# Key-value sums with one column of ones for three heads, and warm-up products that read a preset constant

## The chip, the cores and the metric

The kernel runs on one core of one Trainium2 chip. The metric is the device time of one execution in microseconds (us). It computes, for 2048 tokens of width 640, a layer norm and then the sum of the input, a linear-attention block and a gated feed-forward block. All runs told of here are of the fast state, with a granted clock of 1.000 as recorded.

## The reference, cut to what matters

```python
xn  = layernorm(x)                                   # x: 1 x 2048 x 640, bf16
q, k, v = split(xn @ wqkv)                           # 32 heads of 20
phi_q = concat(softmax(q @ w_phi), softmax(-q @ w_phi))   # 40 features a head
phi_k = concat(softmax(k @ w_phi), softmax(-k @ w_phi))
kv = einsum("bhsf,bhsd->bhfd", phi_k, v)             # the key-value sums
z  = einsum("bhsf->bhf", phi_k)                      # their denominators
o  = (phi_q . kv) / (phi_q . z + 1e-6)
return x + o @ wo + (silu(xn @ w1) * (xn @ w3)) @ w2
```

## The kernel before

The program lists its instructions as streams (norms, projections, gated layer, outputs and so on). A list scheduler inside the program places them with estimated costs. What counts here are the key-value sums and the opening, which is about the first 7 us. An evacuation is the copy of a product's result out of the accumulators by ScalarE or VectorE. An idle product is one whose result nobody reads; it only keeps TensorE active.

A chunk of the sums is 120 feature rows, three heads of 40, and a product gives it the values of its three heads. To get `z` by the same product, each head's 20 values have a column of ones as their 21st. A chunk is therefore 63 columns wide, and there are 11 chunks by 16 row tiles = 176 products. The mask `FM` then keeps, for each row, only the block of its own head.

```python
v2 = new("v2", [128, T, H * 21], bf, RV)
...
memset("POOL", v2[:].rearrange("p t (h c) -> p t h c", c=21)[:, :, :, DH], 1.0)   # the ones
...
def keep_warm(n, rep, rate=2400):          # products that nobody reads
    for _ in range(rep):
        mm(bank(7, 128 * n), zero[:], zero[:].unsqueeze(1).to_broadcast([128, n, 128]), True, True,
           cost=128 * n / rate)

def warm_up():
    keep_warm(4, 8, 1200)
    keep_warm(1, 9, 1200)
...
def v_half(t, q, lo, hi):                  # values of one of the first four row tiles, half q
    ...
        mm(bank(k, 320), xnT[:, i, t * 128:(t + 1) * 128], WVK[:, i, 320 * q:320 * q + 320],
           i == 0, i == DC - 1)
...
def kv_sum(half, k):
    c0, c1 = ((0, 6), (6, QC))[half]
    for c in range(c0, c1):
        n = min(63, H * 21 - 63 * c)
        for t in range(T):
            m = min(128, (T - t) * 1280 - 120 * c)
            f = ekt[:].rearrange("p t f -> p (t f)")[:, 1280 * t + 120 * c:1280 * t + 120 * c + m]
            mm(bank(k, n, 63 * (c - c0))[0:m, :], f, v2[:, t, 63 * c:63 * c + n],
               t == 0, t == T - 1, True, 0.03)
    ...                                    # multiply by FM into KVc, add the epsilon
```

`zero` is a tile that VectorE clears as its first instruction, so the first idle product waits for VectorE.

The softmax here doesn't subtract the row's maximum and nothing guards it: scores larger than these inputs give would overflow.

## Time and profile before

| | before |
|---|---|
| time, median of 3 runs (range) | 266.49 us (266.28 to 266.64) |
| span in the profile | 265.3 us |
| TensorE busy | 259.9 us, 98% |
| VectorE, ScalarE, GpSimd busy | 69%, 40%, 36% |
| first idle product, first transpose | 1.05, 5.68 us |
| key-value products, first to the next other product | 81.37 to 86.48 us |

In a timeline each line has the start in us, the duration, the engine, the operation with what it writes and reads, the count, and in brackets the idle time before it and what ended that. PE is TensorE, and PEld its weight loads. The prediction below shows the lines of this kernel.

### The profile page before, as it was taken

The numbers are of one execution on the slowest core, as the hardware profiler recorded it, in microseconds if no ns is written. First come the engines' busy times: TensorE is split into PE (matmuls) and PEld (weight loads), VectorE is DVE, ScalarE is ACT, GpSimd is POOL, SyncE is SP. The second block draws the span as 40 slices with busy tenths as digits, with TensorE's granted clock in tenths as the row PEclk, the third lists the DMA queues.
The fourth block names the chain that finished last, engine by engine and source line by source line (L and its number), as shares of the span: only waits on it lengthen the run. The fifth ranks groups of instructions, "written<-read, shape, count | busy, mean of one in ns | idle before, by whom it ended". The sixth has DMA issues, their size and how long they took to land.

```text
span 265.3 us, 4446 instructions
## 1 busy us (share of the span) xinstructions
PE 259.9 (98%) x1764; PEld 145.5 (55%) x1792; DVE 183.9 (69%) x316; ACT 106.2 (40%) x226; POOL 95.9 (36%) x107
## 2 busy tenths in 40 slices
PE   7999999999999999999999999999999999999997
PEld 3555545565558556466565745555554544444773
DVE  4668999999796679696675858897979664221112
ACT  5646988799870442251405224434540410000000
POOL 4311587989997035207030430442333020000000
DMA  6996068822300990921515078445751540463431
GB/s 220 284 315 176 4 160 237 174 52 52 121 2 16 260 214 20 158 52 53 107 25 104 2 133 150 57 79 102 123 94 25 101 79 0 93 127 125 104 126 49
DMA packets 72069, 29.03 MB, mean 109 GB/s; under 512 B 60272, under 2 KB 72048, under 8 KB 72048
## 3 DMA queue, kind: packets, MB, share of 16 engines
q1 hardware_dynamic: 71904, 28.58, 47.8%
q8 instruction: 14, 0.23, 0.4%
q10 hardware_dynamic: 144, 0.16, 0.2%
q14 instruction: 7, 0.06, 0.1%
HBM read 11.49 MB, written 2.62 MB: 53 GB/s over the span
## 4 chain that ended last, share of the span: by engine, by line
PE 96%; DVE 1%; DMA 1%; issue 1%; POOL 0%
PE PS L104 96%; DMA x_tok<-in_A_x_dram 1%; DVE bst L104 1%; DVE x_tok L104 0%; POOL rstd L104 0%; DVE mv L104 0%; DVE xres L104 0%; DVE xnT L104 0%
## 5 line engine op out<-in xcount | busy, mean ns | idle before, releaser
L104 PE MATMUL PS<-xnT,w_s 128*128 128x512 bf16 x463 | 105.6, 379 | 1.0 <-issue 0.2
L104 PEld LDWEIGHTS PS<-xnT,w_s 128*128 128x128 bf16 x480 | 46.2, 98 | 50.9 <-DVE xnT L104 0.3
L104 POOL TENSOR_TENSOR eqt<-eqt,rS 128x600 bf16<-128x600 bf16 (+1 forms) x32 | 41.1, 1306 | 91.1 <-DVE rS L104 91.1
L104 ACT ACTIVATE th<-PS 128x512 f32<-128x512 f32 x48 | 28.6, 595 | 68.0 <-PE PS L104 67.9
L104 DVE SCALAR_TENSOR_TENSOR t<-th,PS 128x512 bf16<-128x512 f32 x48 | 32.2, 672 | 25.3 <-ACT th L104 25.3
L104 PE MATMUL PS<-WVK,xnT 128*128 128x512 bf16 (+3 forms) x255 | 45.1, 329 | 0.3
L104 POOL TENSOR_TENSOR ekt<-ekt,rS 128x640 bf16<-128x640 bf16 x32 | 39.8, 1276 | 4.9 <-DVE rS L104 4.9
L104 ACT ACTIVATE eqt<-PS 128x240 bf16<-128x240 f32 (+1 forms) x96 | 27.2, 348 | 25.9 <-PE PS L104 24.1
L104 PEld LDWEIGHTS PS<-WVK,xnT 128*128 128x128 bf16 x260 | 24.1, 98 | 19.4 <-ACT WVK L104 0.4
L104 DVE SCALAR_TENSOR_TENSOR hT<-t,PS 128x512 bf16<-128x512 bf16 x48 | 33.0, 687 | 1.7
L104 PE MATMUL PS<-w_s,hT 128*128 128x320 bf16 (+2 forms) x192 | 27.5, 299 | 0.0
L104 PE MATMUL PS<-hT,w_s 128*128 128x512 bf16 x115 | 27.3, 379 | 0.3
L104 DVE TENSOR_REDUCE S<-ekt 128x64 f32<-128x1280 bf16 x16 | 23.3, 1455 | 2.2 <-ACT ekt L104 2.2
L104 DVE TENSOR_REDUCE S<-eqt 128x66 f32<-128x1320 bf16 x16 | 24.2, 1515 | 0.4 <-ACT eqt L104 0.4
L104 PE MATMUL PS<-Wqp,xnT 128*128 128x360 bf16 (+1 forms) x160 | 24.3, 299 | 0.0
L104 ACT ACTIVATE ekt<-PS 128x640 bf16<-128x640 f32 x32 | 22.3, 702 | 1.3 <-PE PS L104 0.8
L104 PEld LDWEIGHTS PS<-w_s,hT 128*128 128x128 bf16 x192 | 18.3, 98 | 7.8
L104 DVE TENSOR_TENSOR xT<-PS,xT 128x512 bf16<-128x512 f32 x10 | 6.9, 689 | 22.0 <-PE PS L104 22.0
L104 PEld LDWEIGHTS PS<-hT,w_s 128*128 128x128 bf16 x120 | 11.7, 98 | 14.2
L104 PEld LDWEIGHTS PS<-Wqp,xnT 128*128 128x128 bf16 x160 | 15.2, 98 | 7.6
L104 DVE RECIPROCAL rS<-S 128x64 f32<-128x64 f32 (+1 forms) x32 | 17.9, 560 | 1.1
L104 DVE TENSOR_TENSOR xres<-PS,xres 128x640 bf16<-128x640 f32 (+2 forms) x9 | 6.7, 744 | 17.1 <-PE PS L104 17.1
(55 smaller groups left out, 176.9 us busy)
## 6 DMA issues: line engine op xcount, KB each, us to landing
w_s<-in_B_w_dram SPq DMA_DIRECT2D x6, 640.0 KB, 6.4
x_tok<-in_A_x_dram SPq DMA_DIRECT2D x3, 640.0 KB, 5.2
w_s<-in_B_w_dram SPq DMA_DIRECT2D x1, 1920.0 KB, 8.9
out_dram<-ot SPq DMA_DIRECT2D x2, 640.0 KB, 4.7
out_dram<-xres SPq DMA_DIRECT2D x7, 160.0 KB, 1.9
wo_s<-in_A_wo_dram SPq DMA_DIRECT2D x1, 800.0 KB, 5.0
WVK<-in_A_wqkv_dram SPq DMA_DIRECT2D x2, 320.0 KB, 4.0
xres<-in_A_x_dram SPq DMA_DIRECT2D x4, 160.0 KB, 5.8
```

The costliest lines, as they stand in the source:

```text
L104: o = _Op(eng, lambda: m(*args, **kw), r, w, cost)
```

## The change

The intent is to save two columns in each key-value product and to start TensorE without waiting for VectorE. A chunk gets one column of ones in front and then 3 x 20 values, so 61 columns. The mask copies the one denominator to its three heads' places. As a chunk must not straddle two evacuations, the halves of the value projection become 300 + 340 columns, and chunk 10 gets an evacuation of its own. The idle products read a constant that the preamble sets; there are three more of them. The scheduler gets conditions that keep an output behind the load that it adds to.

```diff
-    v2 = new("v2", [128, T, H * 21], bf, RV)
+    v2 = new("v2", [128, T, QC * 61], bf, RV)
+    v2c = v2[:].rearrange("p t (c n) -> p t c n", n=61)
...
-        memset("POOL", v2[:].rearrange("p t (h c) -> p t h c", c=21)[:, :, :, DH], 1.0)
+        memset("POOL", v2c[:, :, :, 0], 1.0)
...
+    one = nc.const_aps.tensor(1.0, [128, 512], bf)
...
-            mm(bank(7, 128 * n), zero[:], zero[:].unsqueeze(1).to_broadcast([128, n, 128]), True, True,
-               cost=128 * n / rate)
+            mm(bank(7, 128 * n), one[:, 0:128], one[:, 0:128 * n], True, True, cost=128 * n / rate)
...
-        keep_warm(1, 9, 1200)
+        keep_warm(1, 12, 1200)
...
+    VH = (0, 300, D)
...
+        if q:
+            evac(v2c[:, t, 10, 1:41], bank(k, 40, 300))
...
-            n = min(63, H * 21 - 63 * c)
+            n = 61 if c < QC - 1 else 41
...
-                mm(bank(k, n, 63 * (c - c0))[0:m, :], f, v2[:, t, 63 * c:63 * c + n],
-                   t == 0, t == T - 1, True, 0.03)
+                mm(bank(k, n, 61 * (c - c0))[0:m, :], f, v2[:, t, 61 * c:61 * c + n],
+                   t == 0, t == T - 1, True, 0.029)
...
-            stt(o[:, :, :, DH], i[:, :, :, DH], DEN_EPS / 2, m, ALU.add, ALU.mult)
+            stt(o[:, :, :, DH], i[:, :, 0].unsqueeze(2).to_broadcast([128, b - a, g]), DEN_EPS / 2, m,
+                ALU.add, ALU.mult)
...
-                    while done["o"] < t + 4 or done["h"] <= b:
+                    while done["o"] < t + 4 or done["h"] <= b or not done["x", b]:
```

More of the change, by code (lines that the diff above doesn't have):

```diff
@@ L546, in fold_mm @@
         evac(dst.rearrange("p (b c) -> p b c", c=320), bank2(k, 320))
+    VH = (0, 300, D)
     def v_out(t, q, k):
-        o = v2[:, t, 336 * q:336 * q + 336].rearrange("p (h c) -> p h c", c=21)[:, :, 0:DH]
-        i = bank(k, 320).rearrange("p (h c) -> p h c", c=DH)
+        o, i = v2c[:, t, 5 * q:5 * q + 5, 1:61], bank(k, 300).rearrange("p (c n) -> p c n", n=60)
         if t < 2 or t == 2 and q == 0:
@@ L561, in v_half @@
         for i in range(lo, hi):
-            mm(bank(k, 320), xnT[:, i, t * 128:(t + 1) * 128], WVK[:, i, 320 * q:320 * q + 320],
+            mm(bank(k, VH[q + 1] - VH[q]), xnT[:, i, t * 128:(t + 1) * 128], WVK[:, i, VH[q]:VH[q + 1]],
                i == 0, i == DC - 1)
@@ L572, in v_first @@
             for q in range(2):
-                mm(bank(2 + q, 320), xnT[:, i, 0:128], WVK[:, i, 320 * q:320 * q + 320], i == 0, i == DC - 1)
+                mm(bank(2 + q, VH[q + 1] - VH[q]), xnT[:, i, 0:128], WVK[:, i, VH[q]:VH[q + 1]],
+                   i == 0, i == DC - 1)
         if hi == DC:
@@ L594, in vk_features @@
                 mm(bank(k + q, hi - lo), xnT[:, i, t * 128:(t + 1) * 128], WVK[:, i, lo:hi], i == 0, i == DC - 1)
-        act(v2[:, t, :].rearrange("p (h c) -> p h c", c=21)[:, :, 0:DH],
-            PS[:, 512 * k:512 * k + D].rearrange("p (h c) -> p h c", c=DH), ACT.Copy)
+        act(v2c[:, t, :, 1:61], PS[:, 512 * k:512 * k + 660].rearrange("p (c n) -> p c n", n=60), ACT.Copy)
         k_exps(t, 512 * k + D)
@@ L650, in kv_sum @@
             o = KVc[:, c0 + a:c0 + b, 0:21 * g].rearrange("p c (g d) -> p c g d", d=21)
-            i = bank(k, 21 * g * (b - a), 63 * a).rearrange("p (c g d) -> p c g d", g=g, d=21)
+            i = bank(k, 61 * (b - a - 1) + 1 + DH * g, 61 * a)
             m = FM[:, a:b, 0:g]
-            tt("DVE", o[:, :, :, 0:DH], i[:, :, :, 0:DH], m.unsqueeze(3).to_broadcast([128, b - a, g, DH]), ALU.mult)
-            stt(o[:, :, :, DH], i[:, :, :, DH], DEN_EPS / 2, m, ALU.add, ALU.mult)
+            if b - a > 1:
+                i = i.rearrange("p (c n) -> p c n", n=61)
+            else:
+                i = i.unsqueeze(1)
+            tt("DVE", o[:, :, :, 0:DH], i[:, :, 1:1 + DH * g].rearrange("p c (g d) -> p c g d", d=DH),
+               m.unsqueeze(3).to_broadcast([128, b - a, g, DH]), ALU.mult)
+            stt(o[:, :, :, DH], i[:, :, 0].unsqueeze(2).to_broadcast([128, b - a, g]), DEN_EPS / 2, m,
+                ALU.add, ALU.mult)
     def q_tok(t, k):
@@ L738, in bass_parallel_sum__linear_kernel_hedgehog__glu_gated_swiglu__prompt_kernel @@
     done = dict.fromkeys(("w", "ln", "t", "f", "k", "v", "n", "kv", "p", "pn", "pt", "q", "o", "h", "m", "first", "t0"), 0)
-    done.update({("u", b): 0 for b in range(NB)})
+    done.update({(k, b): 0 for k in "ux" for b in range(NB)})
+    done["x", 0] = 1
     landed, pace, force = {}, [0], [False]
@@ L929, in outs @@
                 continue
-            while done["o"] <= t or done["h"] <= b:
+            while done["o"] <= t or done["h"] <= b or not done["x", b]:
                 yield None
@@ L938, in turns @@
         yield lambda: load_xT(1)
+        done["x", 1] = 1
         for b in xT:
@@ L945, in turns @@
                 yield lambda: P.dma("SP", xres[:], x_t[:, T - 4:T, :])
+                done["x", 3] = 1
             yield lambda b=b: store(b)
@@ L951, in late_loads @@
         yield lambda: load_xT(2)
+        done["x", 2] = 1
     def set_held(d):
```

## The prediction

> **What bounds the kernel now.** I read the page first: busy shares, then the chain that ended last.
>
> ```profile
> PE 259.9 (98%) x1764; PEld 145.5 (55%) x1792; DVE 183.9 (69%) x316; ACT 106.2 (40%) x226; POOL 95.9 (36%) x107
> ...
> PE 96%; DVE 1%; DMA 1%; issue 1%; POOL 0%
> ```
>
> TensorE is busy 98% of the span of 265.3 us, and the chain is TensorE for 96% of it. VectorE at 69% comes next, so only TensorE time, or time before TensorE's work can start, shortens the run. Busy time is no proof of full speed, however, because a matmul's record includes its pipeline latency. So I next read the chain in order of time, at its start and its end.
>
> ```profile
> 0.80 2.48 DMA x_tok<-in_A_x_dram
> ...
> 4.36 0.23 DVE mv L104
> ...
> 4.67 0.57 POOL rstd L104
> ...
> 6.69 0.36 DVE x_tok L104
> ...
> 7.09 4.56 PE PS L104 x41
> ...
> 258.86 4.58 PE PS L104 x33
> ...
> 263.46 0.29 DVE xres L104
> ```
>
> Up to 7.09 us the chain is the load of the first rows of x and their layer norm (DMA, VectorE, GpSimd, VectorE). From 7.09 to 263.44 it is TensorE without a break that matters: 256.35 us. Then come one addition and the last store.
>
> How close is that stretch to what TensorE can do? I take N/2.4 GHz + 2.5 ns from start to start (source below) and count the program's products: 480 of the gated layer by 215.8 ns = 103.6; values and keys 4.9 + 5.4 + 32.5 (4.9 being the 36 products of 320 columns left after 7.09, by 135.8); queries 80 x 271.7 ns = 21.7; outputs 36.7 + 32.3 + 4.6; weight folding 3.2; transposes 0.8; and about 5.0 each for the key-value sums and their readout. The sum is 255.7 us, plus some 0.17 us of latency of the last one. Against 256.35 us that leaves about 0.5 us of stalls in the whole stretch. No reordering can gain more than that 0.5 us.
>
> **The stages of the change**, in the timeline and in the views of the tiles:
>
> ```profile
> 0.37 0.10 POOL L1032 MEMSET const-bfloat16-1.0<- 128x1 bf16 x1
> ...
> 0.88 0.11 DVE L104 MEMSET zero<- 128x64 uint32 x1 [0.88 <-PEq L1032]
> ...
> 1.05 3.97 PE L104 MATMUL PS<-zero 128*128 128x512 bf16 x17 [1.05 <-DVE warm L104]
> ...
> 5.68 0.28 PE L104 MATMUL PS<-ident,x_tok 128*128 128x128 bf16 x2 [0.66 <-DVE x_tok L104]
> ...
> 81.37 5.27 PE L104 MATMUL PS<-v,ekt 128*128 128x63 bf16 x176
> ...
> 86.45 1.25 PEld L104 LDWEIGHTS PS<-Wqp,xnT 128*128 128x128 bf16 x10
> 86.48 1.52 PE L104 MATMUL PS<-Wqp,xnT 128*128 128x360 bf16 x10
> ```
>
> The idle products start at 1.05 us, when VectorE has written their zeros, and end at 5.02; the first useful one (a transpose) starts at 5.68, on VectorE's layer norm. The 176 key-value products fill 81.37 to 86.48 us: 5.11 us, with no gap at either edge.
>
> **What the Trainium skill says.** (1) "TensorE: Matmul & The Clock Gate", section "Wait — 56ns, not 53.3ns?": start to start N/1.2 GHz cold, N/2.4 GHz + about 2.5 ns warm, and never below about 25 ns. The trace agrees: the cold idle products of 512 columns start at 1.45, 1.88, 2.31 and 2.73 us, 0.43 apart. Of the key-value products, the 42-column ones (the last chunk) start some 25 ns apart (instants 86.09 and 86.29 read 8 products apart by that step), and the other 160 take (5.11 - 16 x 0.0253) / 160 = 29.4 ns against 63/2.4 + 2.5 = 28.8. So at 63 columns the width still counts, barely; at 42 the floor rules. (2) Same page, "What's actually happening": the clock opens after about 3.4 us of activity, in a window that runs freely. Here the 8th wide product, from 4.01 us, is already shortened: the gate opened around 4.3, 3.3 us after the first product. (3) "ScalarE: Activation LUTs", "What ACT_TABLE_LOAD costs": an ACTIVATE takes 186 ns + 0.833 N. The trace: 205 ns at 40 columns (page: 219), 438 at 320, 706 at 640.
>
> **The change part by part.**
> - Key-value products. 160 of 63 columns become 61, 16 of 42 become 41. The first saves 160 x 2 / 2.4 GHz = 0.133 us. The second saves nothing, being at the floor. TensorE is on the path here, so the 0.13 us is real, though only 0.05% of the run.
> - Masking. The two large multiplications (533 and 407 ns), the small one and the three sums of the denominators keep their element counts; only the strides and a repeated operand change. Nothing waits for them at once: the first reader of the result starts at 89.8 us, 2.2 us after the last. 0.
> - Value projection. For four row tiles the halves become 300 + 340 columns: 640 either way, so TensorE 0. Each second half needs one more evacuation of 40 columns, about 0.2 us on ScalarE or VectorE, four in all; the main one shrinks by 20 elements (17 ns). The other twelve copies take 660 columns instead of 640: 12 x 17 ns = 0.2 us on ScalarE, which is at 40%.
> - Ones. GpSimd's write of 512 strided elements takes 2.37 us; 176 elements cost about 0.8 by proportion. GpSimd is not waited for here. 0.
> - Idle products. They read a constant of the preamble, written by 0.47 us, so TensorE need not wait for VectorE: a start at about 0.8 to 0.85. Eight cold wide ones then end near 4.2, and twelve narrow ones (three more) by about 5.0 if warm, 5.5 if still cold. That is before 5.68, so they delay nothing. They gain nothing directly either: 5.68 is set by x and the layer norm, and the clock is full by then in this trace.
> - Order. The program places instructions by a simulated schedule with its own cost estimates. Those of the key-value products fall by 176 x 1 ns, the idle products end 0.04 us earlier in it by my count, and new evacuations appear, so the order may change after the opening. The new conditions before the outputs only keep an output from being placed ahead of the load it adds to.
>
> Sum: -0.13 us for the sums, about +0.1 for evacuations in the opening, -0.1 as the share of executions where an earlier, longer warm-up helps, and order between -0.3 and +0.4: about -0.2, so 266.3 us.
>
> **Rivals.**
> - The four small evacuations collide with the opening. There ScalarE and VectorE are close to the path: between 7.09 and 11.83 us TensorE has about 0.4 us of small stalls (0.15 on x_tok, 0.18 on xnT, about 0.3 before 11.83, part of it hidden). Each extra 0.2 us ahead of a copy of xnT can reach TensorE. For: ScalarE's value copies run without a break from 8.26 to 9.52, and a copy of xnT follows at once. Against: two of the four fall behind other work. Worst case +0.4: 266.7.
> - The clock. If the window opens one step earlier because the products start 0.25 us sooner, executions that open late gain up to about 1 us. For: three runs from 266.28 to 266.64. Against: the clock is already full at 5.68 here, and a start 0.25 us earlier matters in about 0.25/3.4 = 7% of phases. It would make 266.0 at most.
> - The order comes out worse, with TensorE waiting for a release of a bank or a late load. Against: VectorE and ScalarE have slack after the opening. It would make 267 to 268.
> - The products are bound by the weight load and not by their columns. Against: 42-column products with the same 128-column weights are 4 ns quicker. Then the gain is 0: 266.4.
>
> **Range and chances.** The certain part is -0.13, the limit for reordering gains is 0.5 us, runs of one kernel spread by 0.36 us, and the opening can lose 0.4. That gives 265.8 to 266.9. A change of 2% is 5.3 us; nothing here reaches it short of a broken schedule. Faster 0.005, within 2% 0.985, slower 0.01.
>
> **What would show it.** The key-value products should take about 4.97 us from the first to the product after them. The first idle product should start near 0.8, with the first transpose still at 5.7 and the chain entering TensorE near 7.1. TensorE's stretch from there should be about 256.2 us. I am wrong if that stretch moves by over 0.6 us, if the transposes move from 5.7, or if the sums stay at 5.1.

## The result, and the profile after

| | before | after |
|---|---|---|
| time, median of 6 runs (range) | 266.47 us (266.28 to 266.99) | 266.32 us (266.17 to 266.65) |
| span in the profile | 265.3 us | 265.1 us |

The ratio is 0.9994, with a 95% interval from 0.9981 to 1.0006. Ratios are the mean time of one kernel's fast runs over that of the other's of the same rounds, so not quite the ratio of the medians quoted. The interval allows anything from 0.5 us faster to 0.2 us slower. The traces, however, can be compared much more finely than the times.

First the busy line and the chain's shares on the page of the changed kernel:

```profile
PE 260.2 (98%) x1767; PEld 145.7 (55%) x1795; DVE 183.8 (69%) x318; ACT 106.9 (40%) x228; POOL 94.4 (36%) x107
...
PE 96%; DMA 1%; issue 1%; DVE 1%; POOL 0%
```

The bound is as it was. Next the chain in order of time (start, duration, what):

```profile
0.81 2.44 DMA x_tok<-in_A_x_dram
...
6.04 0.91 PE PS L104 x7
6.95 0.03 issue
6.99 4.58 PE PS L104 x41
...
258.65 4.58 PE PS L104 x33
...
263.25 0.29 DVE xres L104
```

The second tile's transposes start at 6.99 us in place of 7.09, and the last addition at 263.25 in place of 263.46. So of the 0.21 us, 0.10 came before this point and 0.11 after it. The chain shows seven products ahead of 6.99 where before it showed VectorE. Both are ways back through nearly simultaneous events, and nothing rests on that.

Now the timeline of the stages that the change touches:

```profile
0.84 4.32 PE L104 MATMUL PS<-const-bfloat16-1.0 128*128 128x512 bf16 x20 [0.84 <-PEq L1047]
...
5.63 0.29 PE L104 MATMUL PS<-ident,x_tok 128*128 128x128 bf16 x2 [0.47 <-DVE x_tok L104]
...
74.90 0.89 POOL L104 MEMSET v<- 128x176 bf16 x1
...
81.26 5.16 PE L104 MATMUL PS<-v,ekt 128*128 128x61 bf16 x176
...
86.27 1.52 PE L104 MATMUL PS<-Wqp,xnT 128*128 128x360 bf16 x10
```

TensorE begins at 0.84 us, but the first useful product still follows the layer norm: 5.63. The sums take 86.27 - 81.26 = 5.01 us against 5.11. The order on TensorE is the same in both kernels, by the names of what its 1774 weight loads outside the idle products read; only the widths and the three more idle products differ.

Here are the landmarks of every profiled run, in us from the start of the span. "x" is the start of VectorE's first statistics, which the load of x releases; "tile 2" is the first transpose of the second tile; "sums" and "next" are the first key-value product and the product after the last one; "end" is the last addition. The last four columns are differences of the rounded instants, so 0.01 us in them means nothing.

| run | x | tile 2 | sums | next | end | x to tile 2 | tile 2 to sums | sums to next | next to end |
|---|---|---|---|---|---|---|---|---|---|
| before | 3.31 | 7.09 | 81.37 | 86.48 | 263.46 | 3.78 | 74.28 | 5.11 | 176.98 |
| after | 3.26 | 6.99 | 81.26 | 86.27 | 263.25 | 3.73 | 74.27 | 5.01 | 176.98 |
| e1 sums only | 3.12 | 6.94 | 81.22 | 86.23 | 263.21 | 3.82 | 74.28 | 5.01 | 176.98 |
| e2 opening only | 3.17 | 7.43 | 81.70 | 86.82 | 263.80 | 4.26 | 74.27 | 5.12 | 176.98 |
| e3 wide sums | 3.16 | 6.88 | 81.16 | 90.12 | 267.10 | 3.72 | 74.28 | 8.96 | 176.98 |
| e4 narrow sums | 3.16 | 6.88 | 81.16 | 85.62 | 262.60 | 3.72 | 74.28 | 4.46 | 176.98 |
| e5 no idle products | 3.17 | 7.31 | 83.10 | 88.11 | 265.09 | 4.14 | 75.79 | 5.01 | 176.98 |
| e6 nine | 3.14 | 6.87 | 81.14 | 86.15 | 263.13 | 3.73 | 74.27 | 5.01 | 176.98 |
| e7 evacuations twice | 3.13 | 6.85 | 81.13 | 86.14 | 263.12 | 3.72 | 74.28 | 5.01 | 176.98 |
| e8c fill | 3.17 | 6.89 | 83.29 | 88.30 | 263.12 | 3.72 | other order | 5.01 | other order |

Two of the four stretches are fixed to 0.01 us wherever the order is the same and the clock is open. So a kernel's time is the arrival of x, the opening, the sums and two constants.

### The profile page after: what moved, and what is told of

Same layout as the page of the kernel before. It is cut to its first block, busy times and chain, and to the rows that moved or that the text cites. A ratio compares the mean times of both kernels' runs of the same rounds, so it can differ in the third digit from the quotient of the medians.

```text
span 265.1 us, 4459 instructions
## 1 busy us (share of the span) xinstructions
PE 260.2 (98%) x1767; PEld 145.7 (55%) x1795; DVE 183.8 (69%) x318; ACT 106.9 (40%) x228; POOL 94.4 (36%) x107
## 4 chain that ended last, share of the span: by engine, by line
PE 96%; DMA 1%; issue 1%; DVE 1%; POOL 0%
PE PS L104 96%; DMA x_tok<-in_A_x_dram 1%; DVE bst L104 0%; POOL rstd L104 0%; DVE mv L104 0%; DVE x_tok L104 0%; DVE xres L104 0%
## 5 line engine op out<-in xcount | busy, mean ns | idle before, releaser
L104 PE MATMUL PS<-WVK,xnT 128*128 128x512 bf16 (+4 forms) x255 | 45.1, 329 | 0.3
```

Of the source, the lines that this page charges most:

```text
L104: o = _Op(eng, lambda: m(*args, **kw), r, w, cost)
```

## The experiments

My theory: the sums are paid by their width down to a floor, that alone is gained, and the opening is set by the arrival of x and the layer norm. The rivals: the gain (if any) is the opening's; the weight load paces the sums; the small evacuations cost time in the opening; the idle products matter otherwise than thought. On TensorE, e1 to e7 keep the order of both kernels (but for the widths and the number of idle products); e8c changes it.

### e1 and e2: the two parts apart

```diff
 e1 (to the kernel after)
-            mm(bank(7, 128 * n), one[:, 0:128], one[:, 0:128 * n], True, True, cost=128 * n / rate)
+            mm(bank(7, 128 * n), zero[:], zero[:].unsqueeze(1).to_broadcast([128, n, 128]), True, True,
+               cost=128 * n / rate)
-        keep_warm(1, 12, 1200)
+        keep_warm(1, 9, 1200)
 e2 (to the kernel before)
 the same two edits the other way round, with the line that defines `one`
```

> The sums in 61 columns, the opening as before. Theory (the two parts are independent, and only the narrower products save): products of the sums from the first to the product after them 5.01 us as in the changed kernel against 5.11 before, first idle product at 1.05, first transpose at 5.6 to 5.7, time 0.10 us under before. Rival (the gain of the changed kernel lies in the earlier opening): time as before within 0.05 us.

> The opening's idle products on the preset constant, twelve narrow ones, the sums in 63 columns as before. Theory (the opening is set by the load of x and the layer norm): sums 5.11 us, first idle product at 0.84, the first transpose within 0.06 us of the instant that follows from this run's own arrival of x plus 2.37 us (before 3.31 to 5.68, changed 3.26 to 5.63), time as before within 0.1 us. Rival (the earlier start or warmer clock brings TensorE's work forward): transposes start sooner after the arrival of x, time 0.1 to 0.2 us under before.

Measured: e1 266.39 us (266.26 to 266.44), ratio 1.0001 (0.9989 to 1.0014); e2 266.44 us (266.40 to 266.86), ratio 1.0005 (0.9991 to 1.0018); the kernel before in the same rounds 266.37 us (266.10 to 266.54; e3 and e4 share these). The times separate neither part from nothing. e1's expected 0.10 us is inside its interval and so is zero.

The traces do separate them. The sums take 5.01 us in e1 and 5.12 in e2, as the theory had it. e2's opening, in the timeline:

```profile
0.84 4.85 PE L104 MATMUL PS<-const-bfloat16-1.0 128*128 128x512 bf16 x20 [0.84 <-PEq L1033]
...
5.54 0.40 PE L104 MATMUL PS<-ident,x_tok 128*128 128x128 bf16 x2
...
6.53 0.49 DVE L104 BATCH_NORM_STATS2 bst<-x_tok 128x6 f32<-128x320 bf16 x1 [0.33 <-DMA x_tok<-in_A_x_dram]
...
7.43 0.45 PE L104 MATMUL PS<-ident,x_tok 128*128 128x128 bf16 x5 [0.22 <-DVE x_tok L104]
```

The start at 0.84 brought nothing forward. The first transpose comes 2.37 us after x, as before and after. Then VectorE waits 0.33 us for a later row tile of x to land, and the opening of this very execution is the longest of all with idle products. Its loads are issued as in the other kernels, but this one took 4.8 us from issue to landing where the other nine runs show 3.4 to 4.4, so this is the scatter of the loads. It is larger than everything that the change could give. e1's first transpose, at 5.48 us, missed my expected 5.6 to 5.7 only because x arrived earlier (3.12 + 2.36).

e1 also shows what a clock that opens late costs. There the products of the first value tile still start as at half speed until about 6.5 us (the idle ones 0.107 us apart to their end), and its "x to tile 2" is 3.82 us against 3.72 to 3.73 where the clock was open by then: about 0.1 us. The earlier start is no protection. In e2, which has it, products of 320 columns start at 6.51 and 6.77 us, 0.26 apart, and only the next step is 0.14.

### e3 and e4: what a column costs

```diff
 e3 (to the kernel after): surplus columns, overwritten or never read; the result is right
-                mm(bank(k, n, 61 * (c - c0))[0:m, :], f, v2[:, t, 61 * c:61 * c + n],
+                n2 = min(122, 651 - 61 * c)
+                mm(bank(k, n2, 61 * (c - c0))[0:m, :], f, v2[:, t, 61 * c:61 * c + n2],
 e4 (to the kernel after): too few columns; the result is wrong on purpose
-                mm(bank(k, n, 61 * (c - c0))[0:m, :], f, v2[:, t, 61 * c:61 * c + n],
+                mm(bank(k, 32, 61 * (c - c0))[0:m, :], f, v2[:, t, 61 * c:61 * c + 32],
```

> Ten of eleven chunks read 122 (one of them 102) columns; the surplus is overwritten or never read, the result stays right. Theory (width/2.4 GHz + 2.5 ns each): 144 x 53.3 + 16 x 45.0 + 16 x 25.3 ns = 8.8 us against 5.0, so the time is 3.8 us over the changed kernel, 270.1. Rival (the load of 128 weight columns sets the pace): the sums stay near 5 us and the time at 266.3; a rival between would show some 60 to 65 ns a product, as a load that doesn't fully overlap.

> All sums read 32 columns only: a wrong result on purpose. Theory (a floor of about 25.3 ns from start to start, as the 42-column products had): 176 x 25.3 ns = 4.45 us, 0.56 us less than the changed kernel, 265.75. Rival without a floor: 176 x 15.8 ns = 2.8 us, 2.2 us less. Rival (weight load sets the pace at any width up to 61): 5.0 us, no change.

Measured: e3 270.26 us, ratio to before 1.0148 (1.0134 to 1.0162); e4 265.64 us, ratio 0.9975 (0.9961 to 0.9988). The timelines of e3 and e4:

```profile
81.16 9.12 PE L104 MATMUL PS<-v,ekt 128*128 128x122 bf16 x176
90.12 1.52 PE L104 MATMUL PS<-Wqp,xnT 128*128 128x360 bf16 x10
```

```profile
81.16 4.61 PE L104 MATMUL PS<-v,ekt 128*128 128x32 bf16 x176
85.62 1.52 PE L104 MATMUL PS<-Wqp,xnT 128*128 128x360 bf16 x10
```

e3 adds 144 x 61 + 16 x 41 = 9440 columns and 8.96 - 5.01 = 3.95 us: 0.418 ns a column, close to the 1/2.4 GHz = 0.417 of the prediction. (The sums came out 0.16 us over the expected 8.8, 1 ns a product.) The weight loads are as many and as wide as before, so at these widths they do not set the pace. e4 comes to 4.46 us / 176 = 25.3 ns a product: the floor, met by 0.01 us, where a cost without a floor would have given 2.8 us. The 61 columns of the change stand at (5.01 - 16 x 0.0253) / 160 = 28.8 ns, only 3.5 ns above the floor. So the idea could never have gained more than 160 x 3.5 ns = 0.56 us more, however narrow the chunks; e4 measures just that (5.01 - 4.46 = 0.55). What makes the floor, the weight load or something in the product itself, these runs do not tell: every product of the sums had a fresh load.

### e5 and e6: what the idle products do

```diff
 e5 (to the kernel after)
-        keep_warm(4, 8, 1200)
-        keep_warm(1, 12, 1200)
+        keep_warm(1, 1, 1200)
 e6 (to the kernel after)
-        keep_warm(1, 12, 1200)
+        keep_warm(1, 9, 1200)
```

> The changed kernel with one idle product in place of twenty at the start. Theory (the idle products matter only for the clock): the first transpose still at 5.6 to 5.7, but products run at half speed until some 3.4 us after TensorE's work begins, to about 9 us; 1.4 us of busy work at full speed done at half by then, so the chain enters its steady part 1 to 2.5 us later and the time is 267.3 to 269. Rival (the idle products are useless): time as the changed kernel, 266.3.

> The changed kernel with nine narrow idle products in place of twelve, so that they end about 4.9. Theory (the clock is open before they end, and stays open over the gap to the first transpose): time as the changed kernel within 0.1 us, width of the products after 5.6 as at full clock. Rival (the three more keep the clock open in some executions): a wider scatter of the runs, some 0.3 us or more longer.

Measured: e5 268.18 us (267.42 to 268.52), ratio to before 1.0062 (1.0045 to 1.0079); e6 266.49 us (266.22 to 266.73), ratio 1.0006 (0.9989 to 1.0022); the kernel before in the same rounds, which e7 and e8c share, 266.41 us (266.24 to 266.62). They were run on another chip. e5's timeline, and its line of the view of cores:

```profile
5.54 0.39 PE L104 MATMUL PS<-ident,x_tok 128*128 128x128 bf16 x2 [4.44 <-DVE x_tok L104]
...
6.25 1.27 PE L104 MATMUL PS<-WVK,xnT 128*128 128x300 bf16 x4
...
7.84 2.92 PE L104 MATMUL PS<-WVK,xnT 128*128 128x300 bf16 x11
...
10.61 0.44 PE L104 MATMUL PS<-ident,x_tok 128*128 128x128 bf16 x5
```

```profile
core 0: 266.9 us, clock 1.000
```

The eleven value products take 2.92 us against 1.62 in e6 and e7. In e5 they start 0.25 to 0.28 us apart, as at half speed; by 10.61 the transposes run at full speed. That is 1.9 us lost up to the sums (83.10 against some 81.2), so the idle products are worth having. The half pace lasted until about 10.5 us, some 5 us from the first transpose, where I had expected 3.4 us and about 9. The three more idle products of the change are not seen to do anything: e6's trace has the same opening (3.73 us) and its runs scatter by 0.51 us, the changed kernel's by 0.48. Its median is 0.17 us over the changed kernel's, outside my 0.1 but inside the scatter.

### e7: do the small evacuations collide?

```diff
             evac(v2c[:, t, 10, 1:41], bank(k, 40, 300))
+            evac(v2c[:, t, 10, 1:41], bank(k, 40, 300))
```

> Each of the four small evacuations of 40 columns is made twice. Theory (they lie beside TensorE's work and cost nothing): the stretch from the second tile's transposes to the first gated-layer product stays at 4.73 us and the time as the changed kernel within 0.1 us. Rival (they collide with the copies of the normalised x): the stretch grows by 0.1 to 0.4 us, and the time with it.

Measured: 266.32 us (266.18 to 266.46), ratio to before 0.9996 (0.9981 to 1.0011). The timeline of e7:

```profile
6.85 0.45 PE L104 MATMUL PS<-ident,x_tok 128*128 128x128 bf16 x5
...
11.36 0.82 PE L104 MATMUL PS<-xnT,w_s 128*128 128x512 bf16 x3
```

The stretch from tile 2 to the sums is 74.28 us, as with half as many evacuations, so no cost of theirs is seen. The trace taught something else. The first gated-layer product starts at 11.36 us, 4.51 after tile 2, where I had expected 4.73. The kernel before shows this:

```profile
11.60 0.11 PEld L104 LDWEIGHTS PS<-xnT,w_s 128*128 128x128 bf16 x2 [0.28 <-DVE xnT L104]
...
11.83 2.11 PE L104 MATMUL PS<-xnT,w_s 128*128 128x512 bf16 x9 [0.17 <-issue]
```

There are nine products where the program issues ten, and an idle time with no cause. In the trace of the kernel before, the first record of that group is missing (its weight load stands at 11.60 us, 4.51 after tile 2, as in e7), and 11.83 is the second product: 4.74 us after tile 2, which is e7's 4.51 and one product of 0.22 us. The stall that I read there in the prediction was for the most part no stall.

### e8c: an attempt at the rest of the stalls

```diff
-                for lo, hi in ((0, 3), (3, DC)):
+                for lo, hi in ((0, 2), (2, DC)) if (t, q) == (2, 1) else ((0, 3), (3, DC)):
```

> An attempt to gain what is left: the value products of the third tile split 2 and 3 in place of 3 and 2, which in the program's own ordering puts more value products between the fourth tile's transposes and the first gated-layer product, where TensorE stalls for about 0.2 to 0.3 us. Theory (those stalls are all that is left in the opening): the start of the steady stretch comes up to 0.3 us sooner and the time is 0.1 to 0.3 us under the changed kernel. Rival: the transposes now wait for the layer norm, or the changed order later costs as much: no gain or a loss of up to 0.5 us.

Measured: 266.29 us (266.14 to 266.61), ratio to before 0.9997 (0.9982 to 1.0012). From x to the end it takes 263.12 - 3.17 = 259.95 us against 259.99 in the changed kernel, e6 and e7: 0.04 us, where I had expected 0.1 to 0.3. The stall that it was to fill was for the most part the missing record, so there was little to find. No version with a right result beats the two kernels by more than the scatter.

## Why the prediction was right

The time of 266.32 us lies beside the predicted 266.3, within 265.8 to 266.9, and "within 2%" held. By its steps:

- **The bound.** Right, and stronger than I had put it. Outside the opening and the sums, the changed kernel repeats the one before to 0.01 us in two stretches of 74 and 177 us.
- **Key-value products, -0.133 us.** The mechanism is right, the size a little off: -0.10 us in the trace (5.11 to 5.01), seen again between e1 and e2. I expected 4.97. e3 confirms the price per column and e4 the floor. Between 61 and 63 columns the step is 0.10/160 = 0.6 ns a product where two columns at full price are 0.83. Both widths lie some 3 to 4 ns above the floor; whether its nearness takes the rest was not tested.
- **Masking, ones, copies of 660 columns: 0.** Right. GpSimd's write of the ones fell from 2.37 to 0.89 us (predicted about 0.8), and nothing after it moved.
- **Small evacuations, +0.1 us.** Wrong in size: 0, and 0 again when doubled. The evidence for that term was partly a missing record: the "about 0.3 before 11.83" that the prediction read there is a wrong reading, as e7 shows.
- **Idle products, -0.1 us.** Not confirmed. The start came out as predicted (0.84), the first transpose as predicted (5.63, on the layer norm). e1 shows that a late clock can cost about 0.1 us, so the size was sensible. But e2's clock opened late despite the earlier start, and nine narrow products did as well as twelve. How often each start opens the clock late was not measured: one profile a kernel cannot tell.
- **Order, between -0.3 and +0.4 us.** 0: TensorE's order did not change. The steady stretch took 263.21 - 6.99 = 256.22 us, as predicted (about 256.2).
- **The sum.** It was added up wrongly: -0.13 + 0.1 - 0.1 is -0.13, and with the middle of the order's range, +0.05, it is -0.08. The "about -0.2" does not follow from its terms; they give 266.4 us.

That the stated sum (-0.2) met the difference of the traces (-0.21) is therefore luck, but for the half of it that the sums of the kernel gave, 0.10. The opening gave the other 0.10, and neither part of that is traced to the change. About 0.04 us is the arrival of x (3.31 against 3.26). About 0.06 is the kernel before taking longer from x to tile 2 than the changed one, e3, e4, e6 and e7. The lines of VectorE show where, first before and then after:

```profile
6.00 0.23 DVE L104 COPY xnT<-PS 128x128 bf16<-128x128 bf16 x1
6.19 0.49 DVE L104 BATCH_NORM_STATS2 bst<-x_tok 128x6 f32<-128x320 bf16 x1
```

```profile
5.96 0.22 DVE L104 COPY xnT<-PS 128x128 bf16<-128x128 bf16 x1
6.10 0.48 DVE L104 BATCH_NORM_STATS2 bst<-x_tok 128x6 f32<-128x320 bf16 x1
```

The statistics of the next row tile start 0.19 us after the copy in the kernel before, and 0.14 after it in every other run but e2. In the trace of the kernel before, that row tile landed only at 6.17 us, 0.02 before its statistics start; in e2 it landed at 6.51 and they start at 6.53. In the other runs it had landed by 6.06. So this part, too, is the scatter of the loads.

## What to carry to other kernels

When an engine is busy from the first possible moment to the last, price a change in that engine's own start-to-start times and do not expect more: two columns of 63 in 160 products are 0.1 us, below the scatter of the loads at the start. Compare traces by stretches between landmarks; stretches agreed to 0.01 us where times scatter by 0.4. Before treating an unexplained idle time as a stall, count the records against what the program issues.

## What the Trainium skill lacked or had wrong

- "TensorE: Matmul & The Clock Gate", "Back-to-back issue gap": it gives streams of weight load and matmul about 81 ns per product at 128 columns and 131 at 512. Here products of 122 columns (a few of 102), each with a fresh load of 128 weight columns, took (8.96 - 0.41) / 160 = 53 ns each, and ten of 512 columns (from 15.13 us in the trace before) took 2.32 us with the last one's 0.38, so (2.32 - 0.38) / 9 = 216 ns each. The formula that the page calls isolated is the one that held.
- Same section, its table: about 60 cycles (the 25 ns floor) for 1 to 64 columns. At 32 and 42 columns it was 25.3 ns, but 28.8 at 61 and 29.4 at 63, so the floor ends before 61.
- Same page, "What you observe": a transition around 4 us, +-0.5 us. Here the pace changed between about 2.9 us (e8c) and 5.9 us (e2) after the first idle product, in programs with the same idle products. In e2 the twenty idle products, back to back, were still at half pace (0.107 us apart) at the last, 4.5 us after the first; short gaps follow before the change.
- The TensorE page warns that the gate's events in a trace can be unreliable, but none of the pages read has it that a profile's mean granted clock can leave the gate out: e5's is 1.000 while its value products start 0.25 to 0.28 us apart instead of about 0.13.
